# Two more accumulator banks for chunks 1, 3 and 5, and a priority for the splits of the down weights, in an attention and gated-MLP layer

## The chip, the cores and the metric

The kernel runs on one core of one Trainium2 chip. The metric is the device time of one execution in microseconds; lower is better. Before the change three runs took 1579.36, 1581.74 and 1583.03 us, so the median is 1581.74 us.

## What is computed

One layer over 2048 tokens of width 576, in float32: layer norm, an attention in which each token looks at itself and seven earlier tokens at a distance of two, a residual, a second layer norm, and a gated MLP with 4608 hidden features, with its residual. Cut to what matters:

```python
def _A_ref(x, wqkv, wo):          # H = 32 heads of 18, W = 8, dilation 2
    qkv = (x @ wqkv).reshape(B, S, 3, H, Dh).transpose(2, 0, 3, 1, 4)
    q, k, v = qkv[0], qkv[1], qkv[2]
    ...
    logits = einsum("bhsd,bhswd->bhsw", q, kg) * scale
    attn = softmax(where(mask, logits, -1e9))
    o = einsum("bhsw,bhswd->bhsd", attn, vg)
    return o.transpose(...).reshape(B, S, D) @ wo

def _B_ref(x, w_gate, w_up, w_down):
    g = x @ w_gate; u = x @ w_up
    return (sigmoid(g) * u) @ w_down

h  = x + _A_ref(layernorm(x), wqkv, wo)
h2 = h + _B_ref(layernorm(h), w_gate, w_up, w_down)
```

## The kernel before

**Numbers in two parts.** TensorE multiplies a rounded float32 format here, so `split` (L103) cuts each operand into a high part, a copy by ACT (L104), and a low part, a subtraction by DVE (L105). A product is then three matmuls: high by high, low by high, high by low. So every weight that arrives from DRAM costs ACT and DVE an instruction per piece before TensorE (PE) can use it.

**Stages.** The tokens are four blocks of 512. Up to some 217 us the kernel does the layer norm, the heads and the attention of block 0; then the MLP begins. The MLP runs over items (L1119), numbered by `c`, each a chunk of 128 hidden features: items 0 to 11 are plain chunks of block 0 (`single`, L782), items 12 to 35 are chunks of blocks 0 and 1 together by a scheme of seven products in place of eight (`pair`, L814), items 36 to 47 plain chunks of block 1, and the other 36 are pairs for blocks 2 and 3. The attention of block 1 runs on DVE underneath items 0 to some 9 (`under_first`), its output goes to DRAM and comes back as tiles `oj`, which PE transposes (L146) and multiplies by the output weights (L157) underneath items 10 and 11; the operands of the pairs come out of that (`operands`, `sums`, L279 to L292). The attention of blocks 2 and 3 runs on DVE underneath the pairs.

**A plain chunk.** `single` takes two PSUM banks, `pg` for the gate and `pu` for the up product. It fills `pg` (14 matmuls of 512 columns), ACT takes its sigmoid (L793), it fills `pu` (14 more), and DVE multiplies the two (`hidden`, L766), after which the result is split into `h0h` and `h0l`. The three banks `b1`, `b2`, `b3` are single buffers: `b_tile(0)` is `b1`, `b_tile(1)` is `b2`, `b_tile(2)` is `b3`. A fourth, `bgp`, is used by the background work alone, which takes `b3` and `bgp` in turn (`bg_bank`, L778); it first does so for the transposes of `oj`. The other four banks are the two double-width buffers `dp` of the down products.

**A pair.** The first product goes to `b1`, which ACT copies (L820); the second goes to another bank, which DVE adds (L825) before ACT takes the sigmoid (L826); the third goes onto `b1` again, which ACT copies (L830), and so on. PE must not go on in a bank before the copy out of it is done.

**Weights.** `load_gu` (L700) brings one item's gate, up and down weights into a tile `wg`, of which there are two, so the load for item `c` waits until every reader of item `c`-2's tile is done. `weights` (L712), called at item `c` for item `c`+1, splits the gate and up weights inside a block of priority `HI`, and for a pair first forms their differences (L727, L728, L730). After that block, outside it, it splits the down weights into a tile `d` (L738), of which there are four. `d` is read by the down products (L864), which come 12 at a time between the other products once both chunks of a couple are done.

**Order.** Each engine runs its instructions in one fixed order, written at build time from the dependencies and a priority: that of an instruction is its place in the program, and `tc.high_priority(n)` sets it `n` instructions earlier. `HI` is 400, `HC` is 700 and is used for what comes straight out of PSUM, the gated values among it; `NSTD` is 12. The attention on DVE has no such offset. Loads are issued by SP, whose queue is in order too: the weights (L702), the attention's inputs (L176 to L178) and the tiles `oj` (L707) stand in one line.

Of the kernel before, what the change touches and what calls it, by code (L numbers as in the profile page):

```python
# [15 lines left out]
F32 = mybir.dt.float32  # L16
# [5 lines left out]
P = 128  # L22
# [30 lines left out]
HI = 400  # L53
HC = 700
NSTD = 12
# [5 lines left out]
def kernel(ctx, tc, x, wqkv, wo, wmlp, out):  # L61
# [6 lines left out]
    def ps_pool(name):  # L68
        return tc.tile_pool(name=name, bufs=1, space=bass.MemoryType.PSUM, reuse_waits="tile")
# [28 lines left out]
    def f32(ap):  # L98
        return ap.bitcast(F32)
# [3 lines left out]
    def split(hi, lo, src):  # L103
        act.activation(hi, src, AF.Copy)  # L104
        splits.append(dve.tensor_tensor(lo, src, f32(hi), ALU.subtract))  # L105
# [585 lines left out]
    gp = ctx.enter_context(ps_pool("gp"))  # L691
# [17 lines left out]
    def d_tile():  # L709
        return gd.tile([P, 2, D], F32R, bufs=4, name="d")  # L710

    def weights(kind, ws, down):  # L712
        with tc.high_priority(HI):
            wd = ws[:, GU:WC]
            r = ws[:, :GU].rearrange("p (c n) -> p c n", c=10)
            w1 = gw.tile([P, 2, 5, P], F32R, bufs=2, name="w1")
            split(w1[:, 0], w1[:, 1], r[:, 5:10])
            w4 = gw.tile([P, 2, 3, P], F32R, name="w4")
            w2 = gw.tile([P, 2, 4, P], F32R, name="w2")
            w3 = gw.tile([P, 8, P], F32R, name="w3").rearrange("p (a n) q -> p a n q", a=2)  # L720
            if kind == "std":
                split(w4[:, 0], w4[:, 1], r[:, 0:3])
                split(w2[:, 0, 0:2], w2[:, 1, 0:2], r[:, 3:5])
                ww = dict(b00=(w1, 0), b10=(w1, 2), b01=(w2, 0))
            else:
                t = gw.tile([P, 8, P], F32, name="tw")
                dve.tensor_tensor(t[:, 2:6], r[:, 1:5], r[:, 3:7], ALU.subtract)  # L727
                dve.tensor_tensor(t[:, 0:2], r[:, 1:3], t[:, 4:6], ALU.subtract)  # L728
                split(w2[:, 0], w2[:, 1], t[:, 0:4])
                dve.tensor_tensor(t[:, 6:8], r[:, 7:9], t[:, 0:2], ALU.subtract)  # L730
                split(w3[:, 0], w3[:, 1], t[:, 4:8])
                split(w4[:, 0], w4[:, 1], r[:, 0:3])
                ww = dict(b00=(w1, 0), b10=(w1, 2), t2=(w2, 0), t3=(w2, 2), t1=(w3, 0), t4=(w3, 2))
            ww.update(g4=(w1, 4), u4=(w4, 0), b11=(w4, 1))
        d = None
        if down:
            d = d_tile()
            split(d[:, 0], d[:, 1], wd)  # L738
        return ww, d

    def prod(ps, xx, w, n, first):
        wt, k0 = w[n]
        k = 0
        for c in range(2):
            for a, m in ((0, 0), (0, 2), (1, 0)):
                pe.matmul(ps, wt[:, a, k0 + c], xx[:, m + c], start=first and k == 0,  # L746
                          stop=k == 5, skip_group_check=True)
                k += 1

    def rest(ps, xx, w, n):  # L750
        wt, k0 = w[n]
        for a in range(2):
            pe.matmul(ps, wt[:, a, k0], xx[:, 4], start=False, stop=a == 1,  # L753
                      skip_group_check=True)
# [10 lines left out]
    def hidden(sg, ps, name):  # L765
        m = dve.tensor_tensor(sg, sg, ps, ALU.mult)  # L766
        gated[0] = getattr(m, "ins", m)
        return halves(name, sg)

    def s_tile():  # L770
        return gh.tile([P, TB], F32, tag="s", bufs=4, name="s")

    def b_tile(i):
        return gp.tile([P, TB], F32, name=f"b{i % 3 + 1}")
# [6 lines left out]

    def single(X, w, t, units, side):  # L782
        xa, xb = (X["a00"], X["a01"]) if t == 0 else (X["a10"], X["a11"])
        pg, pu = b_tile(0), b_tile(1)
        prod(pg, xa, w, "b00", True)
        side(0)
        if c == NSTD - 3:
            units(1)
        prod(pg, xb, w, "b10", False)
        rest(pg, xb, w, "g4")  # L790
        sg = s_tile()
        with tc.high_priority(HC):
            act.activation(sg, pg, AF.Sigmoid)  # L793
        side(1)
        units(1)
        side(2)
        prod(pu, xa, w, "b01", True)
        side(3)
        prod(pu, xb, w, "b11", False)
        rest(pu, xb, w, "u4")  # L800
        with tc.high_priority(HC):
            hid = hidden(sg, pu, f"h{t}")
        side(4)
        if c != NSTD - 3:
            units(1)
        side(5)
        return {t: hid}
# [238 lines left out]
    c = 0  # L1046
# [61 lines left out]
    def units(n):  # L1108
        for _ in range(n):
            while queue:  # L1110
                if next(queue[0], END) is END:
                    queue.pop(0)
                else:
                    break
# [133 lines left out]
    for c, (kind, p, f) in enumerate(items):  # L1248
        w, d = wc
# [18 lines left out]
        if c == 0:  # L1268
            wc = wc_next
        elif c + 1 < len(items):  # L1270
            wc = weights(items[c + 1][0], wg, c + 1 < NF + NSTD)
# [8 lines left out]

        if kind == "std":
            hid = single(X, w, p, late, twice)
        elif not by_seven:
            side = last_pair if c == NF - 1 else bg_step
# [7 lines left out]
        else:  # L1292
# [22 lines left out]
            d = M[f]  # L1315
# [52 lines left out]
```

## Time and profile before

| what | before |
|---|---|
| time, median of 3 runs | 1581.74 us (1579.36 to 1583.03) |
| the profiled execution: its own time | 1584.01 us |
| its span in the trace | 1582.2 us |
| PE busy | 1551.0 us, 98% |
| weight loads of PE busy | 1377.3 us, 87% |
| DVE busy | 1255.2 us, 79% |
| ACT busy | 879.2 us, 56% |
| POOL busy | 199.9 us, 13% |
| chain that ended last | PE 58%, issue 16%, DVE 11%, DMA 8% |

An engine is busy while one of its instructions runs; the ends of matmuls are modelled. In the rows of the timeline, the first column is the start in us, the second the length in us, then engine, line, operation, output and inputs, and in brackets the engine's idle time just before and what ended it. In the rows of waits stand who waited, for whom, the total in us, how often, and the longest. In the rows of the chain stand start, length and what it was.

### The profile page before, as it was taken

The page shows a single profiled execution, that of the slowest core. Times are in us where ns is not written, and L with a number is a line of the kernel's source. Part 1 is how long each engine was busy: PE and PEld are TensorE (multiplying, and loading weights), DVE is VectorE, ACT ScalarE, POOL GpSimd, SP SyncE. Part 2 cuts the span into 40 slices and gives each one's busy share as a digit, 9 for nine tenths or more (in the row PEclk, how much of TensorE's full clock was granted, in tenths as well). Part 3 has the DMA queues.
Part 4 walks back from the last instruction along what each step waited for, and adds up shares of the span by engine and source line. Part 5 has one row for each costly group of instructions (what it writes and reads, how often), then busy time and mean ns, then how long its engine had stood idle before and what let it go on. Part 6 is the DMA issues. An engine that isn't in the chain of part 4 may idle for free.

```text
span 1582.2 us, 22347 instructions
## 1 busy us (share of the span) xinstructions
PE 1551.0 (98%) x8520; PEld 1377.3 (87%) x8520; DVE 1255.2 (79%) x1883; ACT 879.2 (56%) x1584; POOL 199.9 (13%) x249
## 2 busy tenths in 40 slices
PE   8999999999999999999999999999999999999998
PEld 7999888887888888888888888888888888888887
DVE  6998999969999999999426588866777776677755
ACT  6632244435555645566542355766777766777660
POOL 2300000020000010000101010112112112111210
PEclk9999999999999999999999999999999999999999
DMA  8646445365566677664683524999899989999983
GB/s 284 215 168 220 179 185 190 108 235 183 133 167 170 164 176 192 157 162 109 161 242 125 181 81 126 193 181 177 170 180 186 173 173 181 173 173 186 181 169 120
DMA packets 77147, 273.95 MB, mean 173 GB/s; under 512 B 8336, under 2 KB 14224, under 8 KB 76144
## 3 DMA queue, kind: packets, MB, share of 16 engines
q0 software_dynamic: 28192, 107.29, 37.5%
q1 hardware_dynamic: 41216, 145.11, 27.2%
q10 hardware_dynamic: 7632, 20.12, 3.3%
q8 instruction: 66, 1.08, 0.3%
q14 instruction: 41, 0.34, 0.1%
HBM read 143.98 MB, written 130.87 MB: 174 GB/s over the span
## 4 chain that ended last, share of the span: by engine, by line
PE 58%; issue 16%; DVE 11%; DMA 8%; POOL 4%; ACT 2%; SPq 0%; ACTq 0%; POOLq 0%; DVEq 0%
PE b L746 27%; PE dp L864 13%; PE dp L926 6%; PE b L753 5%; PE acc L157 4%; POOL h L935 3%; DMA wg<-in_wmlp_dram 3%; DVE pr L189 2%; DVE pr L215 1%; DVE lg L193 1%; DVE w L105 1%; DVE pr L221 1%; PE b L157 1%; PE bgp L157 1%; DMA x<-tok 1%
## 5 line engine op out<-in xcount | busy, mean ns | idle before, releaser
L746 PE MATMUL b<-tl,w 128*128 128x512 f32 x1704 | 432.6, 393 | 5.1 <-ACT s L820 3.2
L746 PEld LDWEIGHTS b<-tl,w 128*128 128x128 f32 x1704 | 307.9, 188 | 63.6 <-ACT s L820 4.7
L746 PE MATMUL b<-th,w 128*128 128x512 f32 x1344 | 346.2, 392 | 1.5 <-DVE s L839 1.5
L746 PEld LDWEIGHTS b<-th,w 128*128 128x128 f32 x1344 | 244.8, 188 | 46.5 <-DVE s L839 1.9
L932 ACT ACTIVATE ev<-dp 128x576 f32<-128x576 f32 x224 | 144.7, 646 | 63.2 <-PE dp L926 58.9
L753 PE MATMUL b<-th,w 128*128 128x512 f32 x568 | 175.7, 390 | 0.0
L104 ACT ACTIVATE w<-wg 128x384 fp32r<-128x384 f32 (+1 forms) x186 | 110.8, 601 | 111.1 <-PE b L753 48.8
L935 POOL DMA_DIRECT2D h<-ev x128 | 110.0, 860 | 458.6 <-ACT ev L932 444.7
L157 PE MATMUL acc<-qw,th 128*128 128x432 f32 x512 | 154.3, 362 | 2.5 <-DVE th L109 2.3
L105 DVE TENSOR_TENSOR w<-wg,w 128x640 fp32r<-128x640 f32 (+1 forms) x186 | 120.8, 656 | 41.3 <-ACT w L104 41.1
L105 DVE TENSOR_TENSOR w<-tw,w 128x512 fp32r<-128x512 f32 x120 | 82.6, 688 | 82.1 <-ACT w L104 81.5
L753 PEld LDWEIGHTS b<-th,w 128*128 128x128 f32 x568 | 106.5, 188 | 23.2
L864 PE MATMUL dp<-d,h1h 128*128 128x288 f32 x640 | 119.9, 297 | 0.0
L864 PE MATMUL dp<-d,h0h 128*128 128x288 f32 x608 | 114.1, 297 | 0.8 <-DVE tail L874 0.8
L872 ACT ACTIVATE stage<-dp 128x576 f32<-128x576 f32 x104 | 66.9, 645 | 70.1 <-PE dp L864 69.8
L157 PEld LDWEIGHTS acc<-qw,th 128*128 128x128 f32 x512 | 96.6, 189 | 8.4 <-DVE th L109 3.5
L864 PEld LDWEIGHTS dp<-d,h1h 128*128 128x128 f32 x640 | 99.7, 190 | 3.0
L104 ACT ACTIVATE w<-tw 128x512 fp32r<-128x512 f32 x120 | 75.4, 628 | 46.5 <-PE b L746 40.0
L864 PEld LDWEIGHTS dp<-d,h0h 128*128 128x128 f32 x608 | 95.1, 190 | 4.3 <-DVE tail L874 1.0
L157 PE MATMUL acc<-qw,tl 128*128 128x432 f32 x256 | 92.6, 362 | 0.1
L189 DVE TENSOR_TENSOR pr<-kw,q 128x2304 f32<-128x2304 f32 x32 | 81.8, 2556 | 8.8 <-DMA kw<-k 8.7
L880 POOL DMA_DIRECT2D h<-stage x26 | 31.0, 1194 | 436.3 <-ACT stage L872 350.1
(310 smaller groups left out, 2955.5 us busy)
## 6 DMA issues: line engine op xcount, KB each, us to landing
h<-ev POOLq DMA_DIRECT2D x96, 576.0 KB, 7.1
wg<-in_wmlp_dram SPq DMA_DIRECT2D x47, 928.0 KB, 5.9
h<-stage POOLq DMA_DIRECT2D x26, 1152.0 KB, 9.5
wg<-in_wmlp_dram SPq DMA_DIRECT2D x36, 640.0 KB, 4.3
kw<-k SPq DMA_DIRECT2D x16, 792.0 KB, 5.2
vw<-v SPq DMA_DIRECT2D x16, 792.0 KB, 4.3
wd<-in_wmlp_dram SPq DMA_DIRECT2D x18, 576.0 KB, 7.4
h<-ev POOLq DMA_DIRECT2D x32, 288.0 KB, 6.9
```

What stands on the lines that cost most here:

```text
L104: act.activation(hi, src, AF.Copy)
L105: splits.append(dve.tensor_tensor(lo, src, f32(hi), ALU.subtract))
L157: pe.matmul(ps[:, :n], a[:, c, js], m[:, c], start=k == 0, stop=False)
L189: dve.tensor_tensor(pr, both(kw, u), q[:, us].unsqueeze(2).broadcast_to([P, 2, W, CG]), ALU.mult)
L746: pe.matmul(ps, wt[:, a, k0 + c], xx[:, m + c], start=first and k == 0, stop=k == 5, skip_group_check=True)
L753: pe.matmul(ps, wt[:, a, k0], xx[:, 4], start=False, stop=a == 1, skip_group_check=True)
L864: pe.matmul(ps[:, i, :DH2], a[:, js], d[:, m, i * DH2:(i + 1) * DH2], start=k == 0, stop=k == n)
L872: act.activation(hv, ps, AF.Copy)
L880: pool.dma_start(hacc[b], hs, accum_op=ALU.add, max_dma_last_dim=8 * D)
L926: pe.matmul(ps[:, i, :DH2], a[x][:, js], m[y], start=k in (0, 1, 3) and q == 0, stop=q == 2, skip_group_check=True)
L932: act.activation(hs[:, k % 2], ps[:, :, :DH2], AF.Copy)
L935: pool.dma_start(hsev[:, u, k0:k + 1], hs[:, :k + 1 - k0], accum_op=ALU.add, max_dma_last_dim=8 * D)
```

## The change

The split of the down weights, which had no offset, gets one: 400 for every item, and 700 where `weights` is called at items 11 and 12, which is for the down weights of items 12 and 13. And plain chunks 1, 3 and 5 of block 0 put their gate and up products into `b3` and `bgp` instead of `b1` and `b2`. No instruction is added or removed.

```diff
@@ weights
         d = None
         if down:
             d = d_tile()
-            split(d[:, 0], d[:, 1], wd)
+            with tc.high_priority(HC if c in (NSTD - 1, NSTD) else HI):
+                split(d[:, 0], d[:, 1], wd)
         return ww, d
@@ single
         xa, xb = (X["a00"], X["a01"]) if t == 0 else (X["a10"], X["a11"])
-        pg, pu = b_tile(0), b_tile(1)
+        if t == 0 and c < 6 and c % 2:
+            pg, pu = b_tile(2), gp.tile([P, 512], F32, name="bgp")
+        else:
+            pg, pu = b_tile(0), b_tile(1)
         prod(pg, xa, w, "b00", True)
```

## The prediction

> **What bounds the kernel now.** First the page, then the waits of PE, longest first.
>
> ```profile
> span 1582.2 us, 22347 instructions
> PE 1551.0 (98%) x8520; PEld 1377.3 (87%) x8520; DVE 1255.2 (79%) x1883; ACT 879.2 (56%) x1584; POOL 199.9 (13%) x249
> PE mm L497 <- DVE tok L491: 6.6, 1, 6.6
> PE b L146 <- DMA oj<-o: 4.2, 1, 4.2
> PE b L746 <- ACT s L820: 3.2, 3, 2.4
> PE b L746 <- ACT s L830: 1.5, 2, 1.1
> ```
>
> PE is idle for 31.2 us of the span (1582.2 - 1551.0), and 6.6 of them are the start. The change adds and removes no matmul, so a gain can only come out of single waits. The longest two behind the start are 4.2 us for `oj` and 2.4 us for an ACT copy.
>
> **The wait of 2.4 us** is in item 14. Rows of the timelines of ACT, DVE, SP and PE, one of the chain, and one of SP's waits:
>
> ```profile
> 358.52 1.24 ACT L104 ACTIVATE d<-wg 128x576 fp32r<-128x576 f32 x2
> 360.12 0.55 DVE L105 TENSOR_TENSOR w<-wg,w 128x384 fp32r<-128x384 f32 x1
> 368.95 0.75 DVE L105 TENSOR_TENSOR d<-wg,d 128x576 fp32r<-128x576 f32 x1
> 369.77 0.33 SPq L702 DMA_DIRECT2D wg<-in_wmlp_dram  x1
> 378.12 1.29 DVE L105 TENSOR_TENSOR w<-wg,w 128x384 fp32r<-128x384 f32 x2
> 380.85 0.76 DVE L105 TENSOR_TENSOR d<-wg,d 128x576 fp32r<-128x576 f32 x1
> 381.67 8.78 DMA wg<-in_wmlp_dram
> 390.53 0.74 ACT L104 ACTIVATE w<-wg 128x640 fp32r<-128x640 f32 x1 [4.38 <-DMA wg<-in_wmlp_dram]
> 392.68 0.57 ACT L820 ACTIVATE s<-b 128x512 f32<-128x512 f32 x1
> 393.31 4.65 PE L746 MATMUL b<-tl,w 128*128 128x512 f32 x18 [2.37 <-ACT s L820]
> SPq L702 <- DVE d L105: 289.1, 23, 39.1
> ```
>
> ACT splits the down weights of items 12 and 13 at 358.52. DVE does its halves 10 and 22 us later, at 368.95 and 380.85. As long as a half is open, its `wg` is not free: the load for item 14 goes out at 369.77, that for item 15 at 381.67, each right behind a half. The second lands at 390.45 (381.67 + 8.78). ACT stands at its split until then, and the copy of L820, for which PE waits, is behind it on ACT. The last row says how general this is: 23 loads wait for the DVE half of a down split.
>
> **The change part by part.** It moves work and adds none.
>
> *The down splits of items 12 and 13, priority 700.* Their DVE halves can follow ACT's, at some 360 instead of 369 and 381. The tile of item 13 is then held by the next reader, the two weight splits at 378.12, which end at 379.41. So item 15's load goes out at about 379.5 instead of 381.67, 2.2 us earlier; if it takes the same 8.78 us, everything behind it on ACT comes 2.2 us earlier, and PE waits 0.2 instead of 2.37 us: -2.2 us. Next late there is that split, not the load for item 14, which moves up by 9 us.
>
> *The other 44 down splits, priority 400.* The same pattern ended a wait in item 25.
>
> ```profile
> 569.13 0.67 ACT L104 ACTIVATE d<-wg 128x576 fp32r<-128x576 f32 x1
> 572.18 2.55 DVE L189 TENSOR_TENSOR pr<-kw,q 128x2304 f32<-128x2304 f32 x1
> 575.25 0.76 DVE L105 TENSOR_TENSOR d<-wg,d 128x576 fp32r<-128x576 f32 x1
> 576.07 8.34 DMA wg<-in_wmlp_dram
> 585.26 0.82 DVE L105 TENSOR_TENSOR w<-wg,w 128x640 fp32r<-128x640 f32 x1 [1.83 <-ACT w L104]
> 592.27 0.68 DVE L825 TENSOR_TENSOR s<-s,b 128x512 f32<-128x512 f32 x1
> 594.16 1.67 PE L746 MATMUL b<-tl,w 128*128 128x512 f32 x6 [1.15 <-ACT s L830]
> 751.06 0.61 PE L753 MATMUL b<-th,w 128*128 128x512 f32 x2
> 752.14 0.76 DVE L226 TENSOR_TENSOR kw<-kw 128x576 f32<-128x576 f32 x1
> 752.81 0.76 DVE L105 TENSOR_TENSOR d<-wg,d 128x576 fp32r<-128x576 f32 x1
> 753.48 0.69 DVE L825 TENSOR_TENSOR s<-s,b 128x512 f32<-128x512 f32 x1
> 755.36 1.66 PE L746 MATMUL b<-tl,w 128*128 128x512 f32 x6 [0.40 <-ACT s L830]
> ```
>
> DVE's half at 575.25 can follow ACT's at some 570, so the load of 576.07 goes out 5 us earlier, and DVE does not stand idle for 1.83 us at 585.26. The add of L825 then comes up to 1.83 us earlier, which covers PE's 1.15: -1.15 us. Around 752 the half at 752.81 and the add L825 now both outrank the attention's add at 752.14 (0.67 us from start to next start); with that one behind it L825 is 0.67 us earlier, more than PE's 0.40: -0.4 us.
>
> What do these halves push back? DVE is full while the attention runs, so each moves an attention step by 0.67 us. Two places could feel it. Rows of DVE, ACT, PE and the windows:
>
> ```profile
> 307.78 0.75 DVE L226 TENSOR_TENSOR kw<-kw 128x576 f32<-128x576 f32 x1
> 308.45 1.42 DVE L105 TENSOR_TENSOR d<-wg,d 128x576 fp32r<-128x576 f32 x2
> 309.46 6.85 DMA o<-kw
> 319.42 1.11 PE L146 MATMUL b<-ident,oj 128*128 128x128 f32 x4 [4.23 <-DMA oj<-o]
> 361.19 1.22 DVE L285 TENSOR_TENSOR ar<-ar,ar 128x1024 f32<-128x1024 f32 x1
> 363.55 0.50 PE L746 MATMUL b<-tl,w 128*128 128x512 f32 x1 [0.44 <-ACT tl L104]
> 319.00:324.00 5.00, 4.58 (x21) 4.55 (x22) 1.38 (x2) 1.19 (x2) 0.00 (x0) 0.50 1.02 379
> 390.00:394.00 4.00, 1.63 (x8) 1.05 (x7) 0.88 (x2) 3.47 (x7) 0.00 (x0) 1.00 0.00 0
> ```
>
> The two halves at 308.45 stand just behind the attention's last add and can now come ahead of it: the output of block 1 then leaves 1.35 us later, and the 4.23 us wait grows by up to that. It could also shrink to nothing if PE gets more matmuls ahead of the transposes; that end is a rival below. And the halves of items 12 and 13, now near 360, stand ahead of the subtraction at 361.19, for whose result PE waits 0.44 us at 363.55: between nothing and +1.35. I take nothing for both. PE's order is written anew with the same splits in front of the same steps, so more of the down products should stand ahead of the late operand; there are 48 of them for each couple of chunks and block. Both ends stay in the range.
>
> *The banks.* In items 0 to 9 PE waits twice:
>
> ```profile
> PE dp L864 <- DVE h0l L105: 0.9, 1, 0.9
> PE dp L864 <- ACT h0h L104: 0.2, 1, 0.2
> ```
>
> Neither is for a bank. Both are for a split of the gated values, which other banks do not bring earlier. At best they both go (-1.1 us) because the order around them changes; at worst the longer one appears at each of the three chunks moved (3 x 0.9 = +2.7). The background takes `b3` and `bgp` first at 319.42, long after item 5. I take nothing, nearest to what the rows show.
>
> **The sum**: -2.2 - 1.15 - 0.4 = -3.75 us. Of the profiled execution's own 1584.01 us (1.8 outside its span) that leaves 1580.3. That execution is 2.3 us above the median of the runs, 1581.74, against which I count: **1578.0 us**, -0.24%.
>
> **Rivals.**
>
> *The halves stand in front of the add (slower).* In a pair, PE goes on in `b1` only after L825, L826 and L830. Around 752, L825 could start at 751.67 (751.06 + 0.61) and started 1.81 us later; PE lost 0.40. So PE's cover is 1.41 us, and two halves in a row are 1.35. Two down splits become ready together, once per two chunks, just before such an add; 12 times in items 12 to 35. Until now attention steps (2.55 us at 572.18) mostly went first and the halves came later. If in six of those 12 places the cover is already used by an attention step, each costs 1.35: 1578.0 + 8.1 = 1586.1 us. It decides from the point where an attention step and two halves come between PE's release and L825. Against it: the add has priority 700, above the halves, so a half goes first only where it is ready earlier.
>
> *The wait for `oj` falls out of the slow clock (faster still).* The rows of 319 to 324 show a granted clock of 0.50 behind the wait of 4.23 us; five microseconds of matmuls at half speed lose another 2.5. Behind the 2.37 us wait the clock stayed at 1.00. If the new order puts some 1.9 us of matmuls more ahead of the transposes, the wait falls to 2.37 us and the slow stretch goes too: 1578.0 - 1.86 - 2.5 = 1573.6 us. For it: the bank change and the earlier weights give PE more to do before it. Against it: the attention's end comes later, not earlier. The Trainium skill (TensorE: Matmul & The Clock Gate, What's actually happening) says that the clock halves after an idle window of about 3.4 us, and is full again after as long a busy one; both of these waits agree. By it a cut of 0.83 us would be enough, so 1574.7 us.
>
> *It moves nothing that sets the end.* DVE is full, and what it does earlier it owes elsewhere: the 2.2 us come, the other two do not, and both places above take their 0.67: 1581.74 - 2.2 + 1.35 = 1580.9 us. The title speaks of two splits; with 46 raised, those two have less of a head start than it sounds.
>
> **How the numbers follow.** Forecast 0.42 (own range 1575.5 to 1580), slower 0.27, faster still 0.13, nothing 0.18. About 0.2%, 3.2 us, is what a measurement of this kernel can tell from no change. Most of the forecast's case lies beyond it, a part within: faster 0.36 + 0.13, rounded to 0.50; same 0.06 + 0.16 = 0.22; slower 0.28. The range is 1572.5 to 1586: it takes in the clock case, both +1.35 and most of the slower case, and leaves its upper end out.
>
> **What would show it.** Right: the DVE halves of items 12 and 13 within 2 us of ACT's, the loads of items 14 and 15 near 361 and 379, no wait over 0.3 us in item 14, no row of SP's waits with 289 us on the down splits. For the banks: the same two short waits. Wrong: waits for L830 in several pairs; an `oj` wait of more than 5 us; or a clock of 1.00 where it was 0.50.

## The result, and the profile after

| | before | after |
|---|---|---|
| median of 6 runs | 1582.12 us (1577.12 to 1583.03) | 1571.67 us (1569.74 to 1574.56) |
| after to before, 95% interval | | 0.9938 [0.992, 0.9957] |
| the profiled execution: its own time | 1584.01 us | 1574.56 us |
| its span | 1582.2 us | 1572.8 us |

The kernel is 0.62% faster. The forecast was 0.24% (1578.0 us); the measured time lies 0.8 us below the lower end of its range. Both profiled executions are slower than their medians, by 1.9 and 2.9 us. Line numbers of the functions in question have moved by one to four: L746 is now L747, L820 is L824, L825 is L829, L864 is L868. The first line of the page counts four instructions more than before; the counts of the engines in its second line are the same as before.

First the page of the kernel after, then its waits of PE and one of SP's waits (who waited, for whom; total us, times, longest).

```profile
span 1572.8 us, 22351 instructions
PE 1548.3 (98%) x8520; PEld 1376.3 (88%) x8520; DVE 1257.7 (80%) x1883; ACT 882.5 (56%) x1584; POOL 199.5 (13%) x249
PE mm L497 <- DVE tok L491: 6.7, 1, 6.7
PE b L747 <- DVE s L843: 2.6, 2, 2.3
PE acc L157 <- DVE th L109: 2.3, 2, 1.7
PE b L747 <- ACT s L824: 0.9, 1, 0.9
PE bgp L150 <- DVE rstd L125: 0.8, 1, 0.8
PE b L146 <- DMA oj<-o: 0.4, 1, 0.4
SPq L702 <- DVE d L105: 141.1, 11, 20.2
```

The wait for `oj` has gone from 4.2 to 0.4 us, the waits for the first copy of a pair (before: L820) from 3.2 to 0.9. Loads wait for a DVE half of a down split 11 times where it was 23, and 141 us where it was 289.

To see where the 9.4 us of span come from, both traces are cut at two steps: the MLP's first matmul, and the first sigmoid of the plain chunks of block 1 (item 36). Between them, from the timeline of PE:

| us | before | after | |
|---|---|---|---|
| MLP's first matmul to item 36 | 568.0 | 558.1 | -9.9 |
| of this, PE idle | 10.7 | 3.7 | -7.0 |
| of this, PE busy | 557.3 | 554.4 | -2.9 |
| all the rest | 1014.2 | 1014.7 | +0.5 |

So the gain lies in items 0 to 35, and three tenths of it are not idle time: the same matmuls ran faster. The idle 7.0 are made up as follows: the `oj` wait -3.82 (4.23 to 0.41); item 14 -1.27 (2.37 to 0.86 and 0.24); the waits before of 0.52, 1.15, 0.28 and 0.40 in later pairs, in whose place one of 0.28 stands, -2.07; two short ones in the plain chunks (0.25 and 0.86 to 0.17) -0.94; and new ones of 0.82, 0.12 and 0.14 between 341 and 365 us, +1.08.

The first and largest is the `oj` wait. One row of SP's timeline before, the load of item 11:

```profile
309.27 0.33 SPq L702 DMA_DIRECT2D wg<-in_wmlp_dram  x1
```

Then the timeline of the kernel after (start, length, engine, line, operation, in brackets the idle time before); the row at 304.62 begins with the load of item 11, that at 311.59 is the load of item 12:

```profile
219.79 1.56 PE L747 MATMUL b<-tl,wf 128*128 128x512 f32 x6
291.68 1.42 DVE L105 TENSOR_TENSOR d<-wg,d 128x576 fp32r<-128x576 f32 x2
304.00 0.55 DVE L105 TENSOR_TENSOR w<-wg,w 128x384 fp32r<-128x384 f32 x1
304.62 7.30 SPq L702 DMA_DIRECT2D wg<-in_wmlp_dram  x2
307.80 0.75 DVE L105 TENSOR_TENSOR d<-wg,d 128x576 fp32r<-128x576 f32 x1
308.81 0.75 DVE L226 TENSOR_TENSOR kw<-kw 128x576 f32<-128x576 f32 x1
311.59 0.33 SPq L702 DMA_DIRECT2D wg<-in_wmlp_dram  x1
317.77 0.66 PE L146 MATMUL b<-ident,oj 128*128 128x128 f32 x4 [0.41 <-DMA oj<-o]
```

and in its chain of waits and its windows (PE, weight load, DVE, ACT and POOL busy; granted clock, DMA share, GB/s):

```profile
310.49 4.08 DMA o<-kw
314.64 3.08 DMA oj<-o
...
374.22 10.38 DMA wg<-in_wmlp_dram
```

```profile
317.00:325.00 8.00, 7.59 (x47) 5.96 (x45) 7.38 (x15) 4.18 (x11) 0.00 (x0) 1.00 0.99 380
```

Before, the first of the two halves at 308.45 was that of item 9, and the load of item 11, which needs its tile, went out behind it at 309.27, beside the write of the attention's output (309.46, 6.85 us). Now item 9's half runs at about 292 (the second of the two at 291.68), the load goes out at 304.62 behind a weight split, and the write takes 4.08 us. The attention's last add starts at 308.81 where it was 307.78, behind a half at 307.80. The clock behind the wait, 0.50 before, is 1.00. Before, PE ran at 0.50 from the end of the wait (319.42) to about 324.55, which loses 2.6 us: most of the 2.9 us by which PE is less busy.

The other place, item 14, in the timelines of ACT, DVE, SP and PE after:

```profile
349.91 0.69 ACT L104 ACTIVATE d<-wg 128x576 fp32r<-128x576 f32 x1 [0.89 <-PE dp L868]
351.02 0.67 ACT L104 ACTIVATE d<-wg 128x576 fp32r<-128x576 f32 x1
351.89 0.75 DVE L105 TENSOR_TENSOR d<-wg,d 128x576 fp32r<-128x576 f32 x1
353.16 0.75 DVE L105 TENSOR_TENSOR d<-wg,d 128x576 fp32r<-128x576 f32 x1
354.41 0.33 SPq L702 DMA_DIRECT2D wg<-in_wmlp_dram  x1
374.22 0.33 SPq L702 DMA_DIRECT2D wg<-in_wmlp_dram  x1
384.68 1.15 ACT L104 ACTIVATE w<-wg 128x640 fp32r<-128x640 f32 x2 [1.83 <-DMA wg<-in_wmlp_dram]
385.74 0.58 ACT L824 ACTIVATE s<-b 128x512 f32<-128x512 f32 x1
386.37 1.20 PE L747 MATMUL b<-tl,w 128*128 128x512 f32 x4 [0.86 <-ACT s L824]
```

DVE's halves follow ACT's by 2 us. The load of item 14 goes out at 354.41 instead of 369.77, that of item 15 at 374.22 instead of 381.67. It takes 10.38 us instead of 8.78, ACT stands at its split for 1.83 us instead of 4.38, and PE behind the copy for 0.86 instead of 2.37.

### The profile page after: what moved, and what is told of

Read it like the earlier page. It is cut to its first block, busy times and chain, and to the rows that moved or that the text cites. A ratio compares the mean times of both kernels' runs of the same rounds, so it can differ in the third digit from the quotient of the medians.

```text
span 1572.8 us, 22351 instructions
## 1 busy us (share of the span) xinstructions
PE 1548.3 (98%) x8520; PEld 1376.3 (88%) x8520; DVE 1257.7 (80%) x1883; ACT 882.5 (56%) x1584; POOL 199.5 (13%) x249
## 3 DMA queue, kind: packets, MB, share of 16 engines
q8 instruction: 66, 1.08, 0.3%
## 4 chain that ended last, share of the span: by engine, by line
PE 62%; issue 15%; DVE 11%; DMA 6%; POOL 4%; ACT 2%; ACTq 0%; POOLq 0%; SPq 0%; DVEq 0%
PE b L747 29%; PE dp L868 13%; PE dp L930 6%; PE b L754 5%; PE acc L157 4%; POOL h L939 3%; DMA wg<-in_wmlp_dram 2%; DVE pr L189 2%; DVE lg L193 2%; DVE pr L215 1%; PE b L157 1%; PE bgp L157 1%; DVE w L105 1%; DMA kw<-k 1%; DMA x<-tok 1%
## 5 line engine op out<-in xcount | busy, mean ns | idle before, releaser
L747 PE MATMUL b<-tl,w 128*128 128x512 f32 x1692 | 429.6, 393 | 1.7 <-ACT s L824 0.9
L747 PEld LDWEIGHTS b<-tl,w 128*128 128x128 f32 x1692 | 305.8, 188 | 58.5 <-ACT s L824 1.3
L747 PE MATMUL b<-th,w 128*128 128x512 f32 x1332 | 343.1, 392 | 2.6 <-DVE s L843 2.6
L747 PEld LDWEIGHTS b<-th,w 128*128 128x128 f32 x1332 | 242.7, 188 | 47.7 <-DVE s L843 3.4
L105 DVE TENSOR_TENSOR w<-wg,w 128x384 fp32r<-128x384 f32 (+1 forms) x186 | 120.6, 654 | 37.2 <-ACT w L104 37.1
L868 PE MATMUL dp<-d,h1h 128*128 128x288 f32 x640 | 119.9, 297 | 0.0
L868 PE MATMUL dp<-d,h0h 128*128 128x288 f32 x608 | 112.4, 295 | 0.7 <-DVE tail L878 0.7
L868 PEld LDWEIGHTS dp<-d,h1h 128*128 128x128 f32 x640 | 99.9, 191 | 3.0
L868 PEld LDWEIGHTS dp<-d,h0h 128*128 128x128 f32 x608 | 94.0, 189 | 4.5 <-DVE tail L878 1.0
```

The source lines that it names most:

```text
L868: pe.matmul(ps[:, i, :DH2], a[:, js], d[:, m, i * DH2:(i + 1) * DH2], start=k == 0, stop=k == n)
```

## The experiments

Ratios are to the kernel before on the same chip, with the 95% interval. "MLP stretch" is the time from the MLP's first matmul to item 36 in the profiled execution: 568.0 us before, 558.1 after. There is one profiled execution of each kernel, and this stretch varies from one to the next: with the banks alone, on the order of before, it is 564.3 us.

### The parts of the change, each alone

**The banks alone.** The diff's second part without its first.

> The bank part alone on the kernel before; the down splits keep no offset. Theory A (the down splits bring all of it): within 0.2% of before, some 1582 us, with the oj wait still near 4.2 us, the slow clock behind it, and the 2.4 us wait in item 14. Theory B (the banks give PE more work ahead of the oj transposes): some 1577 us, with the oj wait under 2 us and the clock at 1.00 there.

1581.45 us against 1580.8; 0.9999 [0.9988, 1.0011]. The instructions stand in the order of before on ACT, POOL and SP; on PE and DVE nothing differs but the names of the banks. From the waits of PE of this kernel:

```profile
PE b L746 <- ACT s L823: 3.1, 2, 2.5
PE b L146 <- DMA oj<-o: 3.0, 1, 3.0
```

Both long waits are there. (The `oj` wait is shorter in this execution, in which the write took 5.6 us.) The banks bring nothing that these runs can tell.

**The down splits alone.** The first part of the diff without the second.

> The down-split part alone (400 for all, 700 for items 12 and 13), banks as before. Theory A: the whole gain, some 1571.7 us, 0.994 of before; oj wait near 0.4 us and no slow clock there, item 14's wait under 1 us. Theory B: only what items 12 and later give, some 1577 us, with the oj wait still above 3 us.

1572.27 us against 1580.8; 0.9942 [0.9926, 0.9958]; `oj` wait 0.49 us, MLP stretch 557.6. This is the whole gain.

**700 for items 12 and 13, nothing for the others.**

```diff
-            split(d[:, 0], d[:, 1], wd)
+            with ExitStack() as way:
+                if c in (NSTD - 1, NSTD):
+                    way.enter_context(tc.high_priority(HC))
+                split(d[:, 0], d[:, 1], wd)
```

> Only the two splits that the title names: 700 for the down splits of items 12 and 13, none for the other 44, banks as before. Theory of the prediction (item 14's wait was the load of item 15 held by item 13's split): that wait falls from 2.37 to under 0.5 us and nothing else changes, some 1579.5 us. Rival (these two are beside the point, the 44 others bring the gain): within 0.1% of before, or the 2.2 us are lost again in item 12, where two halves now stand ahead of the operands.

1582.53 us against 1580.8; 1.0009 [0.9995, 1.0023]; MLP stretch 568.3. Two rows of PE's timeline:

```profile
390.68 4.60 PE L749 MATMUL b<-tl,w 128*128 128x512 f32 x18 [1.39 <-ACT s L823]
450.26 1.65 PE L749 MATMUL b<-tl,w 128*128 128x512 f32 x6 [1.65 <-ACT s L833]
```

Item 14's wait is a microsecond shorter (2.37 to 1.39), and a wait of 1.65 us stands further on. The halves of items 14 and 15, not raised here, run one behind the other at 406.61 and 407.62, and so the loads of items 16 and 17 go out at 407.44 and 408.43, one microsecond apart; the second takes 11.3 us. Raising these two alone gives nothing.

**400 for all 46, no 700.**

```diff
-            split(d[:, 0], d[:, 1], wd)
+            with tc.high_priority(HI):
+                split(d[:, 0], d[:, 1], wd)
```

> 400 for all 46 down splits, items 12 and 13 among them, banks as before. If the 700 of items 12 and 13 matters: some 1574 us, slower than the whole down-split part by 2 us, with item 14's wait back above 2 us. If it does not: the same as the whole down-split part, some 1571.7 us.

1572.43 us against 1580.8; 0.9941 [0.9925, 0.9958]; MLP stretch 558.1. The 700 isn't needed, and this simpler edit is as good as the change.

### The front and the back of it

The same edit with a condition, `if c + 1 < NSTD` (400 for items 2 to 11), then `if c + 1 >= NSTD` (400 for items 12 to 47), and in a last run `if c + 1 < 14` (items 2 to 13).

> 400 for the down splits of items 2 to 11 alone, the rest none, banks as before. Theory A (the larger part of the gain is the oj wait and the slow clock behind it, and the early down splits bring both): 0.996 of before, some 1575 us, oj wait under 1 us, clock 1.00 behind it, item 14's wait still near 2.4 us. Theory B (the gain is spread over the waits for weights in the pairs): within 0.2% of before, some 1580 us.

> 400 for the down splits of items 12 to 47 alone, banks as before. Theory A: 0.998 of before, some 1577.5 us: the waits for weights in the pairs go (2.4 in item 14, 1.1 in item 25, 0.4 at 755 us), the oj wait stays at 4 us with the slow clock behind it. Theory B: nearly the whole gain, some 1573 us.

| raised to 400 | ratio | `oj` wait | MLP stretch |
|---|---|---|---|
| items 2 to 11 | 1.0036 [1.0021, 1.0051] | 0.29 | 571.2 |
| items 12 to 47 | 0.9969 [0.9958, 0.998] | 4.41 | 561.0 |
| all | 0.9941 [0.9925, 0.9958] | 0.28 | 558.1 |

The `oj` wait goes with the halves of the plain chunks alone, and these alone make the kernel slower. Rows of PE's and SP's timelines with items 2 to 11 raised, and then of its chain of waits:

```profile
321.55 0.66 PE L146 MATMUL b<-ident,oj 128*128 128x128 f32 x4 [0.29 <-DMA oj<-o]
369.72 0.33 SPq L702 DMA_DIRECT2D wg<-in_wmlp_dram  x1
376.70 0.33 SPq L702 DMA_DIRECT2D wg<-in_wmlp_dram  x1
382.67 2.09 PE L749 MATMUL b<-tl,w 128*128 128x512 f32 x6 [4.01 <-ACT s L833]
411.21 1.34 SPq L702 DMA_DIRECT2D wg<-in_wmlp_dram  x2
433.62 2.69 PE L749 MATMUL b<-tl,w 128*128 128x512 f32 x8 [2.45 <-ACT s L823]
```

```profile
376.70 15.08 DMA wg<-in_wmlp_dram
...
411.21 10.10 DMA wg<-in_wmlp_dram
```

The halves of items 12 and 13 still run late, now at 368.90 and 369.57, next to each other. So the loads of items 14 and 15 go out 7 us apart (before: 12; after: 20), with three loads of the attention between them, and take 10.0 and 15.1 us. The loads of items 16 and 17 go out 1 us apart and take 10.1 and 11.7. PE pays with waits of 4.01, 1.47 and 2.45 us. POOL's accumulating writes run beside these loads too, from 367.56 on; which part of the 10 and 15 us is theirs no run separates.

Is it items 12 and 13 that the front lacks? Raising them as well:

> 400 for the down splits of items 2 to 13 alone, banks as before: the part for items 2 to 11, which lost 0.36% by itself, with items 12 and 13 added. Theory E (by itself that part lost because PE reaches the pairs earlier while the tiles of items 12 and 13 are still held by their down splits, so that the loads of items 14 and 15 go out late and together, 10 and 15 us each): the wait of 4.0 us behind item 14 falls under 1.5 us, and the kernel gains 4 us or more on that part, some 1578 to 1583 us; the later waits in items 16 to 35 stay. Rival F (any late split in the pairs costs the same, these two are not special): the 4.0 us wait shrinks but the later ones take its place, some 1587 us as before.

1578.66 us against 1580.63; 0.9985 [0.9971, 0.9999]; `oj` wait 0.56, MLP stretch 565.1. Rows of its PE timeline, of its chain, and of its windows:

```profile
391.07 1.20 PE L749 MATMUL b<-tl,w 128*128 128x512 f32 x4 [2.97 <-ACT s L823]
```

```profile
379.23 9.04 DMA wg<-in_wmlp_dram
```

```profile
393.00:395.00 2.00, 2.00 (x11) 2.00 (x10) 2.00 (x5) 0.17 (x2) 0.00 (x0) 0.50 0.00 0
```

The slowdown is gone, and between 392 and 591 us no wait over 0.25 us is left; so the early halves of items 12 and 13 are what the front lacked. But item 14 still has a wait, of 2.97 us where theory E said under 1.5, and the clock behind it falls. The profiled execution took 1583.32 us, 4.7 more than the median, so a wait of this length need not be typical. The load of item 15 goes out at 379.23, behind the weight split that starts at 378.60; in the kernel after, the split that releases it starts at 373.64. Counted from the MLP's first matmul (222.20 and 219.79 us) that is 2.55 us later. Why the order written for DVE sets it later here isn't explained; nor are some 1.7 of the 7.0 us by which this stretch is longer than in the kernel after (3.6 are waits of PE, 1.9 of them in item 14; 1.7 the clock).

### What shortens the `oj` wait

Two things differ between before and after here: the load of item 11 doesn't run beside the write, and PE has more matmuls ahead of the transposes. The next four runs change the first and leave the second. (The kernel after does have a load beside the write, that of item 12. It goes out 1.10 us behind the write, at 311.59, and lands at 316.32, and the write still takes 4.08 us.)

Two of them didn't bring about what they were made for. In one the load of item 11 was to be issued, in the kernel before, after the paced load ahead of it:

```diff
+        if c == 9:
+            paced(ws[:, :n], wmlp[f][:, :n])
+            return ws
```

> The kernel before with one transfer moved: the load of item 11's weights stands behind the loads of oj in SP's queue instead of ahead of them. Order on PE, DVE, ACT and POOL as before, no priority changed. Theory C (that load ran over the write of the attention's output, which therefore took 6.85 us instead of some 4.1): the write lands in some 4.1 us, the oj wait falls from 4.2 to some 1.5 us, the clock stays at 1.00, and the kernel gains some 4.5 to 5 us (0.997). Rival D (only the 22 matmuls more ahead of the transposes shorten the wait): no change, wait and slow clock as before.

0.9996 [0.9978, 1.0013]. The load still went out beside the write, the write took 6.90 us and the `oj` wait was 4.41: a repeat of before. In the other, the load of the kernel after was to be issued after the attention's last add:

```diff
-        behind[0] = eng.dma_start(ws[:, :n], wmlp[f][:, :n])
+        with ExitStack() as way:
+            if c == 9:
+                end = ends_of[(1, 3)]
+                way.enter_context(tc.issue_after(getattr(end, "ins", end)))
+            behind[0] = eng.dma_start(ws[:, :n], wmlp[f][:, :n])
```

> The changed kernel with one wait more: the load of item 11's weights waits for the attention's last add, so that it runs beside the write of the attention's output, as it did before the change. Order on all engines as in the changed kernel. Theory C: the write takes some 6.8 us again, the oj wait grows from 0.4 to some 3 us, and the kernel loses 2.7 us, with up to 2.5 more if the clock drops. Rival D: no change.

0.9938 [0.9919, 0.9956]. The load went out at 307.25, ahead of the add, the write took 4.02 us and the `oj` wait was 0.27: a repeat of after. The order of issue that was asked for between the two engines was no wait when the kernel ran: the load started 5 us ahead of the add's end. What does hold a load is an access to its tile, so the next two write one column into it, a copy that the load overwrites.

**The kernel before, the load held until the write is done.** POOL copies a column of the first `oj` tile (the lines that keep that tile in `came` are left out).

```diff
+        if c == 9:
+            pool.tensor_copy(ws[:, 0:1], came[0][:, 0:1])
```

> The kernel before with a real hold: the load of item 11's weights waits for one column copied by POOL from the first tile oj, so it cannot run beside the write of the attention's output. No priority changed; the same 294 + 195 matmuls ahead of the transposes. Theory C (the load slowed the write): the write lands in some 4.1 us instead of 6.85, the oj wait is some 1.5 us instead of 4.2, and the clock stays at 1.00 behind it. Rival D (only the matmuls ahead count): write and wait as before. For the whole time neither theory says much, since item 11's weights come some 20 us later and the order after it shifts; 1576 to 1584 us.

1584.46 us against 1581.54; 1.0019 [1.0003, 1.0034]. From its chain, its PE timeline and its windows:

```profile
308.66 4.68 DMA o<-kw
...
313.48 3.07 DMA oj<-o
```

```profile
316.60 0.66 PE L146 MATMUL b<-ident,oj 128*128 128x128 f32 x4 [2.20 <-DMA oj<-o]
```

```profile
316.00:320.00 4.00, 3.40 (x18) 3.38 (x19) 1.11 (x2) 1.20 (x2) 0.00 (x0) 0.67 0.97 347
```

**The kernel after, the load brought down onto the write.** DVE copies a column just behind the attention's last add (`ends_of` keeps that add).

```diff
+        if c == 9:
+            end = ends_of[(1, 3)]
+            with tc.issue_after(getattr(end, "ins", end)):
+                dve.tensor_copy(ws[:, 0:1], mhalf)
```

> The changed kernel with a real hold: the load of item 11's weights waits for one column copied by DVE just behind the attention's last add, so it runs beside the write. 304 + 204 matmuls stand ahead of the transposes, 0.7 us less than in the changed kernel. Theory C: the write takes 6 to 7 us, the oj wait 3 to 4 us (0.4 + 2.7 + 0.7), and the kernel is 3 to 6 us slower than the changed one, some 1576 us. Rival D: write some 4 us, wait about 1.1 us, some 1572.5 us.

1576.93 us against 1581.54; 0.9968 [0.9951, 0.9985]. The load runs from 316.64 to 321.72. From the same three views:

```profile
316.27 5.84 DMA o<-kw
...
322.24 2.86 DMA oj<-o
```

```profile
325.15 0.66 PE L146 MATMUL b<-ident,oj 128*128 128x128 f32 x4 [2.70 <-DMA oj<-o]
```

```profile
325.00:329.00 4.00, 3.58 (x23) 2.96 (x24) 1.98 (x3) 1.41 (x3) 0.00 (x0) 1.00 0.99 357
```

Set beside each other, with times counted from the MLP's first matmul (220.49, 220.55, 225.37 and 219.79 us):

| | write starts | takes | `oj` there | PE at the transposes | wait |
|---|---|---|---|---|---|
| before: load beside the write | 88.97 | 6.85 | 98.89 | 94.70 | 4.23 |
| before, load held off | 88.11 | 4.69 | 96.00 | 93.84 | 2.20 |
| after, load brought onto it | 90.90 | 5.84 | 99.73 | 97.08 | 2.70 |
| after | 90.70 | 4.08 | 97.94 | 97.57 | 0.41 |

The load of item 11 beside the write lengthens it by 2.2 us in the one order and by 1.8 in the other. It matters when the load goes out. In all 14 profiled executions here the write took 5.6 to 6.9 us where a weight load went out within 0.4 us of it (6 of them), and 4.0 to 4.7 where none did and the next came at least 1.0 us later (8). What lies between wasn't tried. The order of after brings PE to the transposes 2.4 to 3.7 us later, with 304 to 307 matmuls of the gate and up products ahead of them where there were 294, and 204 of the down products where there were 195; it starts the write 1.7 to 2.8 us later. Each cause alone leaves a wait of 2.2 to 2.7 us; both are needed. Holding the load off in the order of before costs more than it brings: with the load late, the pairs show waits of 2.69, 1.82 and 1.27 us.

### A later wait

Where the transposes of the next blocks begin, PE waits 1.95 us before (ending at 836 us) and 1.87 after (at 825). The load of item 41, in front of it, takes over 9 us; a load of the output weights stands in the same queue. It was moved behind four others in the kernel after:

```diff
-            paced(f32(ww), wscr[0])
+            if b == 1:
+                paced(f32(ww), wscr[0])
...
+                if b == 2 and n == 9:
+                    paced(f32(ww), wscr[0])
```

> The changed kernel with one transfer moved: the second part of the output weights (1440 KB) of blocks 2 and 3 is issued behind the loads of hj instead of ahead of them, so that it no longer runs beside the load of item 41's weights. Nothing else moves. If that load (9.4 us) is what holds ACT and through it the split for which PE waits 1.9 us at 823, then it lands in some 5 us, the wait and the slow clock behind it (0.79 over 823 to 831) go, and the kernel gains 2 to 3.6 us on the changed one: some 1568.5 us. If not, some 1571.7 us.

1572.62 us against 1581.54; 0.995 [0.9935, 0.9965], the same as after. The row of PE's timeline, and one of the DMA issues from 803 to 820 us (size, us to landing):

```profile
824.56 0.66 PE L146 MATMUL b<-ident,oj 128*128 128x128 f32 x4 [1.94 <-DVE tl L105]
```

```profile
h<-stage POOLq DMA_DIRECT2D x1, 1152.0 KB, 14.4
```

The wait stayed, and the load of item 41 still took 9.46 us. So the output weights aren't what it shares the DMA engines with; POOL's accumulating write runs beside it for 14.4 us, and may be, but no run tried that. The slow clock behind the wait is gone in this execution, though the wait is no shorter; it comes and goes between executions (last section).

## Why the prediction was wrong

**The step that failed** is "I take nothing for both", in the paragraph on what the halves push back. It weighed the place at 308.45 for what two halves cost when they come ahead of the attention's last add, from nothing to 1.35 us. That cost came: the add started 1.03 us later, 1.73 counted from the MLP's first matmul. (The other of the two, at 363.55, was next to nothing: 0.44 us before, 0.44 and 0.14 after.) But the halves of items 2 to 11 have two more effects at this place, and these are larger. PE is 2.87 us later at the transposes (94.70 to 97.57), as the rival on the clock had it, in size more than its 1.9. And the load of item 11 no longer waits for a half, so it is over before the write begins; the write is 2.77 us shorter. 2.87 + 2.77 - 1.73, less 0.1 for the `oj` loads, are the 3.8 us. The prediction had the row of the load's cause before it: it said that 23 loads wait for such a half, and traced three of them. It did not ask which load was waiting for the halves at 308.45, and what that load ran beside. Of its signs of being wrong, the last one came: a clock of 1.00 where it was 0.50.

**The slow clock.** The rival with the chance of 0.13 forecast 1573.6 us for the right mechanism, and is 1.9 us from the median. It priced the wait at -1.86 (measured -3.82) and the clock at -2.5 (-2.6). That its time comes so near is in part luck, since it had item 14 0.9 us too large. Its cause was half right: the earlier weights did give PE more to do ahead of the transposes, the banks brought nothing, and the write that got shorter was in neither account. The forecast took the attention's later end as evidence against it, and put no size on PE's new order, which it did name. The Trainium skill (TensorE: Matmul & The Clock Gate, What's actually happening) has the clock fall after one idle window of about 3.4 us; the waits of 4.0 us and above agree; those of 2.20 us (load held off) and 1.95 us (before, at 836 us), with a clock of 0.50 behind them, don't.

**Item 14.** The mechanism was right: both halves about 2 us behind ACT's, both loads earlier. The sizes were not: -2.2 us forecast, -1.27 measured, and waits of 0.86 and 0.24 us left where the prediction expected none over 0.3. The load of item 15 goes out 7.45 us earlier instead of 2.2, since everything ahead of it has moved too, and it takes 10.38 us rather than the same 8.78, which gives part of it back. And the priority of 700 has no part in it (400 for all: 0.9941; 700 for the two alone: 1.0009).

**Item 25 and 755.36.** Forecast -1.15 and -0.4; the waits of 1.15 and 0.40 us are gone, and so are 0.52 and 0.28 that weren't in the sum. With item 25 and its neighbours not raised (only items 2 to 11, or 2 to 13) a wait of 1.65 or 0.91 us stands at that place (602 and 593 us); with all raised there is none.

**The banks at nothing**: right, 0.9999 [0.9988, 1.0011] alone.

**The slower rival**, halves ahead of the add L825 (now L829) and six waits of 1.35 us: no such wait for it is left among the pairs of blocks 0 and 1 over 0.3 us. A slower kernel does exist, by another mechanism: with only items 2 to 11 raised it is 0.36% slower, and raising items 12 and 13 as well takes that away. The long loads for which it waits run beside each other and beside POOL's writes.

**The parts don't add.** Front +0.36%, back -0.31%, both -0.59%. The sum in the prediction was made as if each place could be priced by itself. Here the halves of one couple set when the loads of the next go out, and what these run beside.

## What to carry to other kernels

Where a small split is the last reader of a buffer that a load waits for, its priority decides when that load starts and what it runs beside; follow each such load to the transfer next to it before the edit is priced at nothing. Try such a priority along the whole loop first: here one part alone was slower than none, and the other gave half of the gain. Where a long wait is followed by a slow clock, price the slow stretch with it, and ask of every edit upstream whether it moves the two sides of that wait, since here both had to move.

## What the runs showed of the hardware

**Whether a wait slows the clock isn't a matter of its length alone.** Where the clock fell in the middle of these executions it fell to 0.50, and it stayed there for 3.4 us or for 6.8. Some of the waits of PE, with what stands next to them:

| clock at 0.50 | waits of PE |
|---|---|
| for 6.8 us | 4.23 (before), 4.48 (700 for two items), 4.41 (load issued later) |
| for 3.4 us | 4.41 (items 12 to 47), 4.01 (items 2 to 11), 3.01 (banks alone), 2.97 (items 2 to 13), 2.20 (load held off) |
| not at all | 2.70 (load brought onto the write), 2.37 (before, item 14), 2.45 (banks alone, item 14) |

The wait at the transposes of the next blocks shows it best. It is 1.8 to 2.1 us long in all 14 executions, and a slow stretch of 3.4 us follows in 7 of them. In the kernel after it is 1.87 us, and with the output weights later 1.94 us. The row of PE's timeline of the first (that of the second stands under "A later wait"), and then the windows behind the two waits, in the same order:

```profile
825.24 0.85 PE L146 MATMUL b<-ident,oj 128*128 128x128 f32 x4 [1.87 <-DVE tl L105]
```

```profile
825.00:829.00 4.00, 3.76 (x17) 3.76 (x18) 1.57 (x3) 1.59 (x3) 0.00 (x0) 0.57 0.92 358
825.00:829.00 4.00, 4.00 (x32) 3.98 (x31) 2.42 (x4) 1.46 (x3) 0.00 (x0) 1.00 0.99 392
```

A mean clock of 0.57 over 4 us is 3.4 us at 0.50. What else decides wasn't tried. At the `oj` wait the two orders differ plainly: with the halves of the plain chunks not raised it was 3.0 to 4.5 us and a slow stretch followed in 5 of 5 executions, with them raised it was 0.3 to 0.6 and none followed in 7 of 7 (the two runs that hold the load are left out).

**Two transfers at once.** The attention's output, 128 KB in its later part, took 4.0 to 4.7 us on POOL's queue where no weight load went out within a microsecond of it, and 5.6 to 6.9 where one went out within 0.4 us of it. Weight loads of 928 KB took 4.5 us with nothing else under way (after, items 10 and 11), and 8.8 to 15.1 for item 15 (before, after, items 2 to 11), where POOL's accumulating writes ran beside them and, in the last two, loads of the attention.
